# Attention + bilinear feed-forward on one core: the attention output of batches 2 to 7 is made token by token, in steps spread over units and outputs

## The chip, the cores and the metric

The kernel runs on one core of one Trainium2 chip. The metric is the device time in microseconds (us). Ten runs of the kernel before have a median of 322.74 us (321.78 to 323.73). Engines are named as in the profile: PE (TensorE), DVE (VectorE), ACT (ScalarE), POOL (GpSimd) and SP (SyncE, which here issues DMAs only).

## The reference

```python
# q, k, v: 8 batches, 8 heads, 576 tokens, 64 each; fp32
kv  = einsum('bhsd,bhse->bhde', k, v)
o   = einsum('bhsd,bhde->bhse', q, kv)
rms = sqrt(mean(o * o, axis=-1, keepdims=True) + 1e-6)     # over the 64 of one head
x   = (o / rms * g_norm).transpose(0, 2, 1, 3).reshape(4608, 512)
out = ((x @ w_a) * (x @ w_b)) @ w_out                      # d_ff = 1536; out is fp32, 4608 x 512
```

## The kernel before

The 4608 tokens of x are cut into nine strips of 512, whose limits do not fall on those of the batches of 576. x is kept transposed, features on partitions, in four tiles `xt[p]` of 128 features x 4608 tokens in bf16.

A strip has twelve *units* and four *outputs*. A unit (`class Unit`, `ffn_ab`) makes 128 of the 1536 hidden features for 512 tokens. `part_a` is four matmuls of 512 columns with w_a into one PSUM bank, which ACT copies to SBUF; `part_b` is four matmuls with w_b into another bank, which DVE multiplies by that copy (L273) into the tile `ab`. An output (`ffn_o`) is twelve matmuls of 512 columns for 128 tokens, an eviction by ACT or DVE in turn, and a store issued on SP. The banks of units rotate over 0, 1 and 2; even outputs use bank 3 (`O`).

The order of the work is written by hand: the program issues instructions in the order in which each engine's queue gets them. Strip 0 is preceded by the attention of batch 0 and followed by that of batch 1. In strip s (1 to 6) the attention of batch b = s + 1 is put between units and outputs by `slot(A, s, n)`, called once after unit or output n (n is 0 to 11 for units, 12 to 15 for outputs). Its steps for one batch are:

- `kv` (L158): k transposed times v, forty small matmuls into bank 7, and `kv_out`, two ACT copies that make the block-diagonal `kvb`, two heads in each of four blocks. It comes after unit 5 in strips 1 and 2, after unit 2 in later strips.
- for each of four pairs of heads p: `x` (L235), two matmuls of 288 columns with `kvb` as weights, into banks 4 and 5; `psq` (L205), the square on ACT; one slot later `pss`, two matmuls of 288 columns with a matrix of ones, which sum the squares over each head and spread the sum over its 64 features (L209), and the reciprocal root on ACT (L213); `pst` (L223), two DVE operations that write `xt`.

q reaches the kernel transposed in this way: `load_late(b)` issues, on POOL, the loads of batch b: q in bf16 to a scratch tensor `qs` in DRAM, then k and v to SBUF. Before it stands a copy of one element, `gate` (L126), which waits until the q of the batch before is transposed. `transpose_q(b)` (L141) is one DMA transposition on SP from `qs` to `qT[b % 2]`. `gate_d`, a DMA of one element of v of batch 1, holds back SP until the early loads are through.

`load_late(3)` is called after unit 8 of strip 1, `transpose_q(3)` and `load_late(4)` at that strip's end; in later strips `transpose_q(b + 1)` and `load_late(b + 2)` after unit 8. `transpose_q(2)` comes at the end of the attention of batch 1, behind the stores of strip 0.

Of the kernel before, what the change touches and what calls it, by code (L numbers as in the profile page):

```python
# [8 lines left out]
FP32 = mybir.dt.float32  # L9
BF16 = mybir.dt.bfloat16  # L10
AF = mybir.ActivationFunctionType
# [4 lines left out]
def kernel(  # L16
# [11 lines left out]
    nc = tc.nc  # L28

    B, H, S, D = q.shape  # L30
    d_model = H * D
    n_tok = B * S
    d_ff = moe_w_a.shape[1]
    KC = d_model // 128
    FC = d_ff // 128
    NP = H // 2
    HF = S // 2
    STRIP = 512
# [3 lines left out]
    EC, EP = 6, 96  # L42
# [6 lines left out]
    def sb(shape, dt, name):  # L49
        return pool.tile(shape, dt, name=name, tag=name)  # L50
# [17 lines left out]
    kvs = [sb([128, NP, D], BF16, f"kvs{i}") for i in range(2)]  # L68

    kvb = [sb([128, NP, 128], BF16, f"kvb{i}") for i in range(2)]  # L70
    xt = [sb([128, n_tok], BF16, f"xt{i}") for i in range(KC)]
    abt = [[sb([128, STRIP], BF16, f"ab{i}_{f}") for f in range(FC)] for i in range(2)]
    a_sb = [sb([128, STRIP], BF16, f"asb{i}") for i in range(4)]
    sq = [sb([128, 2, HF], BF16, f"sq{i}") for i in range(3)]
    rs = [sb([128, 2, HF], FP32, f"rs{i}") for i in range(3)]
    o_sb = [sb([128, d_model], FP32, f"osb{i}") for i in range(4)]
    o_end = sb([128, d_model // 2], FP32, "o_end")
    ident = sb([128, 128], BF16, "ident")
# [2 lines left out]
    g_col = sb([128, 1], FP32, "g_col")  # L81
    eps_t = sb([128, 1], FP32, "eps_t")
    warm = sb([128, 1], FP32, "warm")
    k32 = sb([EP, 2, EC, D], FP32, "k32")
    v32 = sb([EP, 2, EC, D], FP32, "v32")
    q32 = sb([EP, 2, EC, D], FP32, "q32")

    qc = sb([EP, EC, 2 * D], BF16, "qc")
    kc0 = sb([EP, EC, 2 * D], BF16, "kc0")
# [5 lines left out]
    P = psum.tile([128, 8, STRIP], FP32, name="P", tag="P")  # L95
    O = 3
# [26 lines left out]
    def load_late(b):  # L123
        if b > EARLY:

            nc.gpsimd.tensor_copy(gate, qT[(b - 1) % 2][0:1, 0, 0:1])  # L126
        d = qs_d[b].rearrange("t (h d) -> t h d", h=H)
        for hs in (slice(0, NP), slice(NP, H)):
            nc.gpsimd.dma_start(out=d[:, hs, :], in_=q[b, hs].rearrange("h t d -> t h d"))  # L129
        n = 128 * LC  # L130
        for t, src in ((ktl[b % 2], k), (vtl[b % 2], v)):
            nc.gpsimd.dma_start(
                out=t[:, :, 0:LC, :],
                in_=src[b, :, 0:n].rearrange("h (t c) d -> t h c d", c=LC),
            )
            nc.gpsimd.dma_start(
                out=t[0 : S - n, :, LC, :], in_=src[b, :, n:].rearrange("h t d -> t h d")
            )

    def transpose_q(b):  # L140
        nc.sync.dma_start_transpose(qT[b % 2], qs_d[b])  # L141


    class Attn:
# [75 lines left out]
        def pst(self, p, x0, hs=(0, 1)):  # L220
            for h in hs:
                t0 = self.b * S + h * HF
                nc.vector.scalar_tensor_tensor(  # L223
                    out=xt[p][:, t0 : t0 + HF],
                    in0=P[:, x0 + h, 0:HF],
                    scalar=g_col,
                    in1=rs[p % 3][:, h, :],
                    op0=ALU.mult,
                    op1=ALU.mult,
                )  # L230
# [10 lines left out]
                )  # L241


    class Unit:
        n = 0

# [5 lines left out]
        def mm(self, w, kcs):  # L252
            t0 = self.s * STRIP
            for kc in kcs:
                nc.tensor.matmul(  # L255
                    self.a if w is wa_t else self.b,
                    lhsT=w[:, kc, self.fc * 128 : (self.fc + 1) * 128],
                    rhs=xt[kc][:, t0 : t0 + STRIP],
                    start=(kc == KORD[0]),
                    stop=(kc == KORD[-1]),  # L260
                )
# [13 lines left out]
        def rest(self, kcs=KORD):  # L275
            self.part_a(kcs)
            self.part_b(kcs)

    n_ab = [0]

    def ffn_ab(s, fc):
        i = n_ab[0]
        n_ab[0] += 2
        Unit(s, fc, i % 3, (i + 1) % 3).rest()

    def store(t0, t, e0, e1, eng=nc.sync):
        i = 0
# [15 lines left out]
    def o_mm(s, g, i, fcs, e0=0, e1=d_model):  # L303
        for fc in fcs:
            nc.tensor.matmul(  # L305
                P[:, i, e0:e1],
                lhsT=abt[s % 2][fc][:, g * 128 : (g + 1) * 128],
                rhs=wo_t[:, fc, e0:e1],
                start=(fc == 0),
                stop=(fc == FC - 1),  # L310
            )

    def o_out(s, g, i):
        n = n_o[0]
        n_o[0] += 1
        t = o_sb[n % 4]
        if n % 2:
            nc.scalar.copy(t, P[:, i, :])  # L318
        else:
            nc.vector.tensor_copy(t, P[:, i, :])  # L320
        store(s * STRIP + g * 128, t, 0, d_model)

    def ffn_o(s, g, i=O):
        o_mm(s, g, i, range(FC))
        o_out(s, g, i)


# [41 lines left out]
    X, SS = (4, 0), 6  # L369


    A = Attn(0)
# [9 lines left out]
    t = P[:, 2, :].bitcast(BF16)[:, 0:S].rearrange("q (c t) -> q c t", c=EC)  # L382
# [4 lines left out]
    for c in range(EC):  # L387
        nc.tensor.matmul(
            P[:, SS, 0 : 2 * D],
            lhsT=kc0[:, c, :],  # L390
            rhs=vc[:, c, :],
            start=(c == 0),
            stop=(c == EC - 1),
# [10 lines left out]
    for p in range(1, NP):  # L404
        i = X[p % 2]
# [34 lines left out]
    u3.part_a()  # L440
    u2.part_b()
    u3.part_b()
    n_ab[0] = 1
    for fc in range(4, FC):
        ffn_ab(0, fc)


    A = Attn(1)
    h1, h2 = range(0, FC // 2), range(FC // 2, FC)

    nc.sync.dma_start(out=gate_d, in_=vt[1][0:1, H - 1, EC - 1, D - 1 : D])
    ffn_o(0, 0, X[0])
    pieces = [(1, h1), (1, h2), (2, h1), (2, h2), (3, h1), (3, h2)]
    for n, (g, fcs) in enumerate(pieces):
# [9 lines left out]
        if n < NP:  # L464
# [1 line left out]
            A.kv1(n, 2)  # L466
            A.kv_out(n, P[:, 2, STRIP - D :])
            A.qtr_out(n, 2)
    transpose_q(2)
    u0 = Unit(1, 0, 2, 3)  # L470
    u1 = Unit(1, 1, 4, 5)
    u0.first((0, 1, 2))
    u1.first((0, 1, 2))
    u0.rest((3,))
    u1.rest((3,))
    n_ab[0] = 0


    def slot(A, s, n):

        kb = P[:, 7, 0 : NP * D].rearrange("q (p e) -> q p e", e=D)
        k0, kn, xs = (5, 1, (7, 9, 11, 13)) if s < 3 else (2, 1, (4, 7, 10, 12))
        if k0 <= n < k0 + kn:
            for p in range((n - k0) * NP // kn, (n - k0 + 1) * NP // kn):
                A.kv(p, kb[:, p, :])
            if n == k0 + kn - 1:
                A.kv_out(slice(0, NP), kb)
        for p in range(NP):
            if n == xs[p]:
                A.x(p, X[0])  # L490
                A.psq(p, X[0])
            if n == xs[p] + 1:
                A.pss(p, SS)
                A.pst(p, X[0])

    for s in range(1, N_STRIP - 1):
        b = s + 1
        A = Attn(b) if b < B else None
        for n in range(FC + 4):
            if n >= FC:  # L500
                i = O if n % 2 == 0 else n_ab[0] % 3
                n_ab[0] += n % 2
                ffn_o(s, n - FC, i)
            elif s > 1 or n > 1:
                ffn_ab(s, n)
            if A:
                slot(A, s, n)
            if n == 8 and b + 1 < B:
                if s > 1:
                    transpose_q(b + 1)  # L510
                    if b + 2 < B:
                        load_late(b + 2)
                else:
                    load_late(3)
        if s == 1:
            transpose_q(3)
            load_late(4)
    last = N_STRIP - 1
    for fc in range(FC):
        ffn_ab(last, fc)  # L520
    for g in range(3):
        ffn_o(last, g, (O, 4)[g % 2])
# [38 lines left out]
```

## Time and profile before

| | |
|---|---|
| median of ten runs | 322.74 us |
| the profiled execution | 322.97 us |
| its span, first to last instruction | 321.2 us |
| granted TensorE clock | 0.999 |
| strips 3, 4, 5, 6: start on PE (us) | 119.97, 153.87, 187.77, 221.67 |
| strip 7 (no attention), strip 8: start on PE | 255.56, 286.64 |
| loads of q, k, v of batch 2: issued on POOL | 41.4 to 48.0 |
| kv step of batch 2 on PE | 61.06 to 62.9 |

The profile is one execution, with times in microseconds from the span's first instruction unless ns is written. A group's row joins instructions of one line of the code, one engine and one operation; `out<-in` are the program's tiles. A timeline's row joins neighbouring instructions of one kind: start, length, what, how many, and in brackets how long the engine had been idle and who ended that. The row of a matmul is longer than the time it keeps the next one waiting, since matmuls overlap. Weight loads (PEld) overlap them too. "q" after an engine's name means its queue, so `SPq` rows are DMA issues.

### The profile page before, as it was taken

The numbers are of one execution on the slowest core, as the hardware profiler recorded it, in microseconds if no ns is written. First come the engines' busy times: TensorE is split into PE (matmuls) and PEld (weight loads), VectorE is DVE, ScalarE is ACT, GpSimd is POOL, SyncE is SP. The second block draws the span as 40 slices with busy tenths as digits, with TensorE's granted clock in tenths as the row PEclk, the third lists the DMA queues.
The fourth block names the chain that finished last, engine by engine and source line by source line (L and its number), as shares of the span: only waits on it lengthen the run. The fifth ranks groups of instructions, "written<-read, shape, count | busy, mean of one in ns | idle before, by whom it ended". The sixth has DMA issues, their size and how long they took to land.

```text
span 321.2 us, 4697 instructions
## 1 busy us (share of the span) xinstructions
PE 312.9 (97%) x1848; PEld 150.6 (47%) x1883; DVE 124.9 (39%) x218; ACT 125.8 (39%) x217; POOL 70.0 (22%) x94
## 2 busy tenths in 40 slices
PE   8899999899999999999999999999999999999995
PEld 3444454444445444444444445444444444444443
DVE  5543344344234433453244323532354243313421
ACT  3733165353335424552355325533454233123310
POOL 8945890070034080160080000000000000000000
PEclk9999999999999999999999999999999999999999
DMA  8999999999359999999799141003000200020002
GB/s 177 196 196 199 200 181 226 142 83 162 89 94 148 147 113 211 102 112 174 142 67 156 65 119 23 0 35 99 0 2 0 98 35 0 23 90 22 0 33 98
DMA packets 79308, 32.60 MB, mean 101 GB/s; under 512 B 49974, under 2 KB 74806, under 8 KB 79286
## 3 DMA queue, kind: packets, MB, share of 16 engines
q0 software_dynamic: 59120, 18.44, 52.7%
q1 hardware_dynamic: 19810, 13.44, 17.8%
q10 hardware_dynamic: 356, 0.43, 0.4%
q8 instruction: 14, 0.23, 0.3%
q14 instruction: 8, 0.07, 0.1%
HBM read 37.75 MB, written 12.98 MB: 158 GB/s over the span
## 4 chain that ended last, share of the span: by engine, by line
PE 79%; DMA 14%; POOL 5%; issue 1%; ACT 0%; POOLq 0%
PE P L255 48%; PE P L305 26%; DMA wb_t<-in_moe_w_b_dram 6%; DMA vtl<-in_v_dram 5%; PE P L235 2%; PE P L209 2%; DMA qt<-in_q_dram 2%; DMA wo_t<-in_moe_w_out_dram 2%; PE P L158 1%; POOL qs L129 1%; POOL vt L106 1%; POOL wo_t L121 0%; POOL wb_t L360 0%; POOL wa_t L360 0%; POOL qt L106 0%
## 5 line engine op out<-in xcount | busy, mean ns | idle before, releaser
L273 DVE TENSOR_TENSOR ab<-P,asb 128x512 bf16<-128x512 f32 x108 | 74.5, 692 | 125.0 <-PE P L255 124.1
L255 PE MATMUL P<-xt,wa_t 128*128 128x512 bf16 x420 | 110.7, 379 | 1.0 <-issue 0.2
L255 PE MATMUL P<-xt,wb_t 128*128 128x512 bf16 x421 | 110.1, 379 | 0.4
L305 PE MATMUL P<-wo_t,ab 128*128 128x512 bf16 (+1 forms) x433 | 97.3, 373 | 0.6
L269 ACT CAST asb<-P 128x512 bf16<-128x512 f32 x108 | 63.1, 587 | 81.7 <-PE P L255 80.2
L255 PEld LDWEIGHTS <-wb_t 128*128 128x128 bf16 x432 | 42.3, 98 | 51.0 <-DMA wb_t<-in_moe_w_b_dram 0.3
L305 PEld LDWEIGHTS <-ab 128*128 128x128 bf16 x444 | 43.0, 98 | 45.6
L255 PEld LDWEIGHTS <-wa_t 128*128 128x128 bf16 x432 | 41.7, 98 | 44.7 <-issue 0.5
L223 DVE SCALAR_TENSOR_TENSOR xt<-P,g_col,rs 128x288 bf16<-128x288 f32 x64 | 30.1, 512 | 24.4 <-ACT rs L213 24.4
L213 ACT ACTIVATE rs<-P,eps_t 128x576 f32<-128x576 f32 (+1 forms) x33 | 23.9, 727 | 20.7 <-PE P L209 16.5
L318 ACT COPY osb<-P 128x512 f32<-128x512 f32 x17 | 10.0, 586 | 48.6 <-PE P L305 46.8
L205 ACT ACTIVATE sq<-P 128x576 bf16<-128x576 f32 x31 | 20.2, 651 | 20.2 <-PE P L235 18.2
L320 DVE COPY osb<-P 128x512 f32<-128x512 f32 x18 | 12.5, 692 | 32.4 <-PE P L305 32.3
L129 POOL DMA_DIRECT2D qs<-in_q_dram x12 | 19.6, 1635 | 2.2 <-issue 2.1
L126 POOL COPY gate<-qT 1x1 bf16<-1x1 bf16 x5 | 0.9, 177 | 85.4 <-DMA qT<-qs 85.4
L209 PE MATMUL P<-sq,ones 128*128 128x288 bf16 x64 | 13.2, 286 | 0.5 <-ACT sq L205 0.4
L235 PE MATMUL P<-qT,kvb 128*128 128x288 bf16 x56 | 11.9, 286 | 0.0
L169 ACT CAST kvb<-P 64x256 bf16<-64x256 f32 (+1 forms) x20 | 6.0, 301 | 12.4 <-PE P L158 12.3
L209 PEld LDWEIGHTS <-ones 128*128 128x128 bf16 x64 | 6.2, 98 | 7.4 <-issue 0.4
L235 PEld LDWEIGHTS <-kvb 128*128 128x128 bf16 x56 | 5.5, 98 | 6.0
L121 POOL DMA_DIRECT2D wo_t<-in_moe_w_out_dram x12 | 6.4, 530 | 6.7 <-DMA wb_t<-in_moe_w_b_dram 3.3
L330 PE MATMUL P<-zeros 128*128 128x512 bf16 x16 | 6.3, 542 | 1.2 <-DVE eps_t L345 1.2
(55 smaller groups left out, 83.7 us busy)
## 6 DMA issues: line engine op xcount, KB each, us to landing
out_dram<-osb SPq DMA_DIRECT2D x23, 256.0 KB, 2.0
qs<-in_q_dram POOLq DMA_DIRECT2D x12, 288.0 KB, 6.9
ktl<-in_k_dram POOLq DMA_DIRECT2D x6, 512.0 KB, 8.9
vtl<-in_v_dram POOLq DMA_DIRECT2D x6, 512.0 KB, 11.3
out_dram<-osb SPq DMA_DIRECT2D x13, 128.0 KB, 2.5
wo_t<-in_moe_w_out_dram POOLq DMA_DIRECT2D x12, 128.0 KB, 6.0
wa_t<-in_moe_w_a_dram POOLq DMA_DIRECT2D x5, 256.0 KB, 9.1
wb_t<-in_moe_w_b_dram POOLq DMA_DIRECT2D x5, 256.0 KB, 9.7
```

Of the source, the lines that this page charges most:

```text
L129: nc.gpsimd.dma_start(out=d[:, hs, :], in_=q[b, hs].rearrange("h t d -> t h d"))
L205: nc.scalar.activation(sq[p % 3], P[:, i0 : i0 + 2, 0:HF], AF.Square)
L209: nc.tensor.matmul(P[:, i0 + h, 0:HF], lhsT=ones, rhs=sq[p % 3][:, h, :], start=True, stop=True)
L213: nc.scalar.activation(rs[p % 3][:, h0:h1, :], P[:, i0 + h0 : i0 + h1, 0:HF], AF.Abs_reciprocal_sqrt, bias=eps_t,)
L223: nc.vector.scalar_tensor_tensor(out=xt[p][:, t0 : t0 + HF], in0=P[:, x0 + h, 0:HF], scalar=g_col, in1=rs[p % 3][:, h, :], op0=ALU.mult, o ...
L235: nc.tensor.matmul(P[:, i0 + h, 0:HF], lhsT=kvb[self.b % 2][:, p, :], rhs=self.qT[:, p, h * HF : (h + 1) * HF], start=True, stop=True,)
L255: nc.tensor.matmul(self.a if w is wa_t else self.b, lhsT=w[:, kc, self.fc * 128 : (self.fc + 1) * 128], rhs=xt[kc][:, t0 : t0 + STRIP], st ...
L269: nc.scalar.copy(self.t, self.a)
L273: nc.vector.tensor_mul(abt[self.s % 2][self.fc], self.b, self.t)
L305: nc.tensor.matmul(P[:, i, e0:e1], lhsT=abt[s % 2][fc][:, g * 128 : (g + 1) * 128], rhs=wo_t[:, fc, e0:e1], start=(fc == 0), stop=(fc == F ...
L318: nc.scalar.copy(t, P[:, i, :])
L320: nc.vector.tensor_copy(t, P[:, i, :])
```

## The change

Of batches 2 to 7, x is made by tokens. A batch has five chunks: four of 128 tokens and one of 64. A chunk c has four steps:

- `tx`: four matmuls of 128 columns, with 128 tokens of `qT` as weights and a block of `kvb` as the moving side. They fill one bank (5, 6 or 7, by c % 3) with tokens on partitions and all 512 features in the columns. ACT squares the bank into `sqt`.
- `tss`: DVE sums the squares of each head: 128 x 512 to 128 x 8.
- `trs`: ACT makes 128 x 8 reciprocal roots; POOL multiplies root and `g_norm`, both broadcast, to 128 x 512 in fp32, over `sqt`.
- `txt`: DVE multiplies the bank by that into a bf16 tile with tokens on partitions; SP issues a DMA transposition of it to `xt`, which is now one tile of 128 x 4 x 4608.

The matmuls with ones and the two DVE operations per pair are no longer used for these batches. A slot is now also called in the middle of a unit, between `part_a` and `part_b`, with n - 0.5, and in the middle of an output. A chunk that starts at x has its steps at x, x + 0.5, x + 1 and x + 2.5. In strip 1 the starts are 6.5, 7.5, 8.5, 9.5 and 10.5; in later strips 3.5, 5, 6, 7.5 and 8.5. kv of batch 3 (strip 2) moves from unit 5 to unit 2.

Units use four banks in turn (4, 1, 2, 0), and odd outputs take from the same rotation. `transpose_q(2)` moves ahead of strip 0's first output, so on SP ahead of that strip's stores; `transpose_q(3)` from the end of strip 1 to its first output; `load_late(3)` from unit 8 to unit 3 of strip 1; the other late loads to n = 13, the second output. Tiles for loads of the first heads (`k32`, `q32`, `v32`) lend their memory to the new tiles.

```diff
+    AB = (4, 1, 2, 0)
     n_ab = [0]
-    def ffn_ab(s, fc):
-        i = n_ab[0]
-        n_ab[0] += 2
-        Unit(s, fc, i % 3, (i + 1) % 3).rest()
+    def ab_bank():
+        n_ab[0] += 1
+        return AB[(n_ab[0] - 1) % len(AB)]
+
+    def ffn_ab(s, fc, between=None):
+        u = Unit(s, fc, ab_bank(), ab_bank())
+        u.part_a()
+        if between:
+            between()
+        u.part_b()
...
+        def tx(self, c, i):
+            t0 = c * 128
+            n = min(128, S - t0)
+            for p in range(NP):
+                nc.tensor.matmul(
+                    P[0:n, i, p * 128 : (p + 1) * 128],
+                    lhsT=self.qT[:, p, t0 : t0 + n],
+                    rhs=kvb[self.b % 2][:, p, :],
+                    start=True,
+                    stop=True,
+                )
+            nc.scalar.activation(
+                sqt[c % 3][0:n], P[0:n, i, :].rearrange("t (h d) -> t h d", h=H), AF.Square
+            )
+
+        def tss(self, c):
+            n = min(128, S - c * 128)
+            nc.vector.reduce_sum(sst[c % 3][0:n], sqt[c % 3][0:n], axis=mybir.AxisListType.X)
+
+        def trs(self, c):
+            n = min(128, S - c * 128)
+            nc.scalar.activation(
+                rst[c % 3][0:n],
+                sst[c % 3][0:n],
+                AF.Abs_reciprocal_sqrt,
+                bias=eps_t[0:n],
+                scale=1.0 / D,
+            )
+            nc.gpsimd.tensor_mul(
+                sqt[c % 3][0:n],
+                rst[c % 3][0:n].unsqueeze(2).to_broadcast([n, H, D]),
+                g_all[0:n].unsqueeze(1).to_broadcast([n, H, D]),
+            )
+
+        def txt(self, c, i):
+            t0 = c * 128
+            n = min(128, S - t0)
+            t = x_tok[c // 3][:, c % 3]
+            nc.vector.tensor_mul(
+                t[0:n], P[0:n, i, :].rearrange("t (h d) -> t h d", h=H), sqt[c % 3][0:n]
+            )
+            t0 += self.b * S
+            nc.sync.dma_start_transpose(
+                xt[:, :, t0 : t0 + n], t[0:n].rearrange("t h d -> t (h d)")
+            )
...
     nc.sync.dma_start(out=gate_d, in_=vt[1][0:1, H - 1, EC - 1, D - 1 : D])
+    nc.sync.dma_start(out=g_all, in_=g_norm.partition_broadcast(128))
+    transpose_q(2)
     ffn_o(0, 0, X[0])
...
-    transpose_q(2)
...
-        k0, kn, xs = (5, 1, (7, 9, 11, 13)) if s < 3 else (2, 1, (4, 7, 10, 12))
+        k0, xs = (5, (6.5, 7.5, 8.5, 9.5, 10.5)) if s == 1 else (2, (3.5, 5, 6, 7.5, 8.5))
...
-        for p in range(NP):
-            if n == xs[p]:
-                A.x(p, X[0])
-                A.psq(p, X[0])
-            if n == xs[p] + 1:
-                A.pss(p, SS)
-                A.pst(p, X[0])
+        for c, x in enumerate(xs):
+            i = 5 + c % 3
+            if n == x:
+                A.tx(c, i)
+            elif n == x + 0.5:
+                A.tss(c)
+            elif n == x + 1:
+                A.trs(c)
+            elif n == x + 2.5:
+                A.txt(c, i)
...
         for n in range(FC + 4):
+            amid = (lambda n=n: slot(A, s, n - 0.5)) if A else None
             if n >= FC:
-                i = O if n % 2 == 0 else n_ab[0] % 3
-                n_ab[0] += n % 2
-                ffn_o(s, n - FC, i)
+                ffn_o(s, n - FC, ab_bank() if n % 2 else O, amid)
             elif s > 1 or n > 1:
-                ffn_ab(s, n)
+                ffn_ab(s, n, amid)
             if A:
                 slot(A, s, n)
-            if n == 8 and b + 1 < B:
-                if s > 1:
-                    transpose_q(b + 1)
-                    if b + 2 < B:
-                        load_late(b + 2)
-                else:
-                    load_late(3)
-        if s == 1:
-            transpose_q(3)
-            load_late(4)
+
+            if s == 1 and n == 3:
+                load_late(3)
+            if b + 1 < B and n == (12 if s == 1 else 8):
+                transpose_q(b + 1)
+            if b + 2 < B and n == 13:
+                load_late(b + 2)
```

More of the change, by code (lines that the diff above doesn't have):

```diff
@@ L70 @@
     kvb = [sb([128, NP, 128], BF16, f"kvb{i}") for i in range(2)]
-    xt = [sb([128, n_tok], BF16, f"xt{i}") for i in range(KC)]
+    xt = sb([128, KC, n_tok], BF16, "xt")
     abt = [[sb([128, STRIP], BF16, f"ab{i}_{f}") for f in range(FC)] for i in range(2)]
@@ L75 @@
     rs = [sb([128, 2, HF], FP32, f"rs{i}") for i in range(3)]
+    k_x = sb([128, 2 * EC * D], FP32, "k_x")
+    k32 = k_x[0:EP].rearrange("p (h c d) -> p h c d", h=2, c=EC)
+    sqt = [sb([128, H, D], FP32, f"sqt{i}") for i in range(2)]
+    sqt.append(k_x[:, 0 : H * D].rearrange("p (h d) -> p h d", h=H))
+    sst = [sb([128, H], FP32, f"sst{i}") for i in range(3)]
+    rst = [sb([128, H], FP32, f"rst{i}") for i in range(3)]
+    g_all = sb([128, D], FP32, "g_all")
     o_sb = [sb([128, d_model], FP32, f"osb{i}") for i in range(4)]
@@ L83 @@
     warm = sb([128, 1], FP32, "warm")
-    k32 = sb([EP, 2, EC, D], FP32, "k32")
-    v32 = sb([EP, 2, EC, D], FP32, "v32")
-    q32 = sb([EP, 2, EC, D], FP32, "q32")
+    qv = [sb([128, 2 * EC * D], FP32, f"qv{i}") for i in range(2)]
+    q32, v32 = (t[0:EP].rearrange("p (h c d) -> p h c d", h=2, c=EC) for t in qv)
+    x_tok = [t.bitcast(BF16).rearrange("p (c h d) -> p c h d", c=3, h=H) for t in qv]
     qc = sb([EP, EC, 2 * D], BF16, "qc")
@@ L223, in pst @@
                 nc.vector.scalar_tensor_tensor(
-                    out=xt[p][:, t0 : t0 + HF],
+                    out=xt[:, p, t0 : t0 + HF],
                     in0=P[:, x0 + h, 0:HF],
@@ L257, in mm @@
                     lhsT=w[:, kc, self.fc * 128 : (self.fc + 1) * 128],
-                    rhs=xt[kc][:, t0 : t0 + STRIP],
+                    rhs=xt[:, kc, t0 : t0 + STRIP],
                     start=(kc == KORD[0]),
@@ L321, in o_out, with ffn_o @@
         store(s * STRIP + g * 128, t, 0, d_model)
-    def ffn_o(s, g, i=O):
-        o_mm(s, g, i, range(FC))
+    def ffn_o(s, g, i=O, between=None):
+        o_mm(s, g, i, range(FC // 2))
+        if between:
+            between()
+        o_mm(s, g, i, range(FC // 2, FC))
         o_out(s, g, i)
@@ L442 @@
     u3.part_b()
-    n_ab[0] = 1
+    n_ab[0] = 0
     for fc in range(4, FC):
@@ L475 @@
     u1.rest((3,))
-    n_ab[0] = 0
+    n_ab[0] = 1
     def slot(A, s, n):
         kb = P[:, 7, 0 : NP * D].rearrange("q (p e) -> q p e", e=D)
-        k0, kn, xs = (5, 1, (7, 9, 11, 13)) if s < 3 else (2, 1, (4, 7, 10, 12))
-        if k0 <= n < k0 + kn:
-            for p in range((n - k0) * NP // kn, (n - k0 + 1) * NP // kn):
+        k0, xs = (5, (6.5, 7.5, 8.5, 9.5, 10.5)) if s == 1 else (2, (3.5, 5, 6, 7.5, 8.5))
+        if n == k0:
+            for p in range(NP):
                 A.kv(p, kb[:, p, :])
-            if n == k0 + kn - 1:
-                A.kv_out(slice(0, NP), kb)
-        for p in range(NP):
-            if n == xs[p]:
-                A.x(p, X[0])
-                A.psq(p, X[0])
-            if n == xs[p] + 1:
-                A.pss(p, SS)
-                A.pst(p, X[0])
+            A.kv_out(slice(0, NP), kb)
+        for c, x in enumerate(xs):
[8 more added lines that the diff above has]
+                A.txt(c, i)
     for s in range(1, N_STRIP - 1):
```

## The prediction

> **What bounds the kernel now.** I read the page's engine shares and costliest groups first. Columns of a group: line, engine, operation, output and inputs, count, then busy us, mean ns of one, then idle us of the engine before them and what ended most of it.
>
> ```profile
> PE 312.9 (97%) x1848; PEld 150.6 (47%) x1883; DVE 124.9 (39%) x218; ACT 125.8 (39%) x217; POOL 70.0 (22%) x94
> ...
> L273 DVE TENSOR_TENSOR ab<-P,asb 128x512 bf16<-128x512 f32 x108 | 74.5, 692 | 125.0 <-PE P L255 124.1
> ...
> L209 PE MATMUL P<-sq,ones 128*128 128x288 bf16 x64 | 13.2, 286 | 0.5 <-ACT sq L205 0.4
> L235 PE MATMUL P<-qT,kvb 128*128 128x288 bf16 x56 | 11.9, 286 | 0.0
> ```
>
> TensorE (PE) is busy nearly all the time; VectorE and ScalarE idle mostly because they wait for it. The waits of PE alone, longest first, say that it waits for almost nothing:
>
> ```profile
> PE P L330 <- DVE eps_t L345: 1.2, 1, 1.2
> PE P L158 <- DMA vtl<-in_v_dram: 0.9, 1, 0.9
> PE P L209 <- ACT sq L205: 0.4, 1, 0.4
> ```
>
> The 0.4 lies in the prologue; the 0.9 is the kv step of batch 2, in strip 1. Nothing waits in the later strips, so there each matmul taken off PE is time gained, until something else becomes late. A table of stretches shows it: strips 5 and 6, which carry attention, and strip 7, which carries none (columns: stretch, its length, busy us and count of PE, weight load, DVE, ACT, POOL, then clock, DMA share, GB/s).
>
> ```profile
> 187.77:221.67 33.90, 33.69 (x198) 16.26 (x201) 13.45 (x22) 14.41 (x24) 0.00 (x0) 1.00 0.18 45
> 221.67:255.57 33.90, 33.69 (x198) 16.28 (x201) 13.45 (x22) 14.41 (x24) 0.00 (x0) 1.00 0.10 36
> 255.57:286.68 31.11, 30.95 (x143) 14.10 (x145) 9.68 (x14) 8.22 (x14) 0.00 (x0) 1.00 0.09 35
> ```
>
> Attention of one batch costs 33.90 - 31.11 = 2.79 us, all of it PE time. The timeline gives the pieces (columns: start, length, engine, line):
>
> ```profile
> 7.06 0.49 PE L388 MATMUL P<-vc,kc 96*128 96x128 bf16 x6
> ...
> 54.14 1.29 DVE L273 TENSOR_TENSOR ab<-P,asb 128x512 bf16<-128x512 f32 x2 [1.46 <-PE P L255]
> ...
> 58.28 1.03 PE L255 MATMUL P<-xt,wb_t 128*128 128x512 bf16 x4
> ...
> 59.42 0.69 DVE L273 TENSOR_TENSOR ab<-P,asb 128x512 bf16<-128x512 f32 x1 [1.04 <-PE P L255]
> ```
> ```profile
> 247.31 0.41 PE L235 MATMUL P<-qT,kvb 128*128 128x288 bf16 x2
> 247.55 2.75 PE L305 MATMUL P<-wo_t,ab 128*128 128x512 bf16 x11
> 250.14 0.41 PE L209 MATMUL P<-sq,ones 128*128 128x288 bf16 x2
> 250.38 5.34 PE L305 MATMUL P<-wo_t,ab 128*128 128x512 bf16 x24
> ```
>
> A matmul's own duration (286 ns) is not its price, since matmuls overlap; the price is the distance to the next start. Two 288-column matmuls take 247.55 - 247.31 = 0.245 us, so 0.1225 each (0.24 for the ones, too). Six 128-column matmuls, each with its own weight load, span 0.49 with a mean of 0.218: five distances of (0.49 - 0.218) / 5 = 0.055. For 512 columns the distance is 1.726 us per unit / 8 = 0.216.
>
> **What the skill says.** "TensorE: Matmul & The Clock Gate", section "Back-to-back issue gap", gives N / 2.4 + 2.5 ns for the distance, which the three numbers above meet within 1 ns; the same section warns of about 81 ns at N = 128 in a stream of load and matmul pairs. The six pairs above say 55; I take 55 and keep 81 as the upper end. "GPSIMD Engine Reference", section "Elementwise — side-by-side cycle accounting", has 4497 ns for a two-input product of 2048 fp32 per partition; a quarter is an estimate of 1.12 us. This trace shows no such operation; the nearest, the mask of 128 elements made on POOL in the prologue (287 ns), gives 1.15 times four.
>
> **The change, part by part.**
>
> *x by tokens.* Removed per batch: 8 x matmuls and 8 matmuls with ones, 16 x 0.1225 = 1.96 us. Added: 5 chunks x 4 matmuls x 0.055 = 1.10 us. Six batches: 6 x 0.86 = 5.16 us off PE (with 81 ns it would be 6 x 0.34 = 2.0). The weight loads grow from 16 to 20 per batch, and hide behind the matmul before, as in the row of six.
>
> *The other engines' work.* Per strip DVE gives up 8 x 0.512 and takes 5 sums and 5 products, each over as many elements as the ab product (0.69): +2.8 on 13.45 in a strip of 33. ACT gives up 4 x (0.651 + 0.742) and takes 5 squares (0.59, as the copies of 128x512) and 5 small roots (0.2, as the first activation): -1.6. POOL takes 5 products, 5.6 us. All of it lies beside PE; it costs only if one step comes too late for the next user of its bank. So I follow the bank chain.
>
> *Strips 2 to 6.* With 0 at the end of part_a of unit 5, ACT has the root at 1.0, POOL's first product ends at 2.2, DVE reaches txt(0) after the product of unit 6, about 3.7: POOL is early by 1.5. tx(3) uses the bank of chunk 0 and stands 1.5 units after txt(0); tx(4) one unit after txt(1), which DVE ends about 1.1 us ahead of it. No wait on PE. The cover is thin only for POOL (below).
>
> *Strip 1.* Here the chunks start at 6.5, 7.5, 8.5, 9.5, 10.5, one unit apart. txt(0) is due at 9, tx(3) at 9.5, only half a unit later, in the same bank. With 0 at the end of unit 9's matmuls: DVE starts the ab product at 0.28 (59.42 less 58.28 + 4 x 0.216), the second operation of a pair follows 0.60 later (1.29 - 0.69), txt(0) ends at 0.28 + 0.60 + 0.69 = 1.57, and PE gets it about 0.06 later. PE is through part_a of unit 10 at 0.86. It stands for 1.63 - 0.86 = 0.77 us, and nothing else can go on PE. tx(4) meets txt(1) in the same way. Two waits: +1.54 us. Bounds: 0 if DVE were far faster, 3 if POOL is late too.
>
> *Earlier transposition of q of batch 2.* In the SP queue it now stands ahead of the eight stores of strip 0's outputs.
>
> ```profile
> 46.68 5.89 SPq L298 DMA_DIRECT2D out_dram<-osb  x8
> ```
> ```profile
> 62.29 0.69 PE L158 MATMUL P<-vtl,ktl 128*64 128x64 bf16 x32 [0.92 <-DMA vtl<-in_v_dram]
> ...
> 63.61 0.18 POOL L126 COPY gate<-qT 1x1 bf16<-1x1 bf16 x1 [15.57 <-DMA qT<-qs]
> 64.45 3.26 POOL L129 DMA_DIRECT2D qs<-in_q_dram  x2 [0.67 <-issue]
> ...
> 70.13 0.72 POOL L136 DMA_DIRECT2D vtl<-in_v_dram  x1
> ```
>
> The transposition started at 53.80, after the stores, though its source was issued by 43.26 with 6.9 us median to landing, so about 50.2. The skill ("Trainium Kernel Development and Optimization", "Key Constraints") has all queues share the same 16 DMA engines; here the v load, issued at 46.4, took 14.7 us against 11.3 for the median of all v loads. With the stores behind, it should land earlier. Of the 0.92 I take 0.7 as gained (between 0 and 0.92). The stores go out by about 66; their buffers are next written at 77.
>
> *Loads of batch 3* (n = 3 instead of 8) follow the gate, thus the transposition, not their place: POOL was idle for 15.57 before. But POOL products now stand behind these issues. Issuing takes 63.61 to 70.85; if the gate opens 3 us earlier it ends by about 67.5, when the first root comes out (unit 8 of strip 1). *Transposition of batch 3* at n = 12: SP reaches it near 79, its source landed by 73; it lands near 85 and the loads of batch 4 are issued by 92, ahead of strip 2's first product near 95. From strip 3 on the transposition of q waits behind two chunk transposes, later by some 10 us; everything it feeds is due a strip later. *kv of batch 3* at unit 2: needed near 90, loaded by 80. Cost 0 each.
>
> *Chunk transposes on SP.* A q transposition of 576 rows took 2.4 to 6.9 us to issue and at most 10.6 to land; a chunk has 128. The tightest is chunk 2 in strip 1, due 10.4 us (four outputs) after unit 11, less 1.6 for DVE. Between 0 and 1.8; I take 0.
>
> *Four ab banks, halves of outputs.* PE did not wait for a bank before; 0.
>
> Sum against the profiled execution (322.97, span 321.2): -5.16 + 1.54 - 0.7 = -4.3, so 318.65; the median of the runs is 0.23 lower, so 318.4.
>
> **Rivals.**
>
> A. No wait in strip 1 (DVE runs earlier than I have it), kv wait gone: 322.74 - 5.86 = 316.9. Against it: three measured durations leave 0.77. Chance 0.08.
>
> B. The gate of batch 3 does not open earlier. POOL issues until 70.85, its first product ends at 71.95, txt(0) at 72.7, while PE stands at tx(3) from 71.4: 1.35 instead of 0.77, and the kv wait stays: -5.16 + 2.12 = -3.0, 319.7. For it: the shared DMA engines are full there. Chance 0.15.
>
> C. 81 ns for each of 120 short matmuls: +3.1 on the forecast, 321.5. For it, the skill's sentence; against it, the row of six. Chance 0.08, half of it within 0.3% of before.
>
> D. Slower: the POOL product is several times its estimate, and DVE stands at txt with the ab products queued behind it. In strips 2 to 6, with 0 as above, txt(1) is through at 1.06 + 2T + 0.75, and PE wants its bank for tx(4) at 7.56 (the matmuls from part_b of unit 5 to part_a of unit 9). PE waits from T = 2.9 us and the batch's gain of 0.86 is gone at T = 3.3; at T = 4 it costs 2.25 x 5 = 11.3 us, thus 329.7. For it: no such product is in the trace, and its inputs are broadcast. Chance 0.10.
>
> **How the numbers follow.** The main case has 0.59. A measurement of this kernel tells about 0.3% (1 us) from no change. Faster: 0.59 + 0.08 + 0.15 + 0.04 = 0.86; within: 0.04; slower: 0.10. The range 316.8 to 320.8 holds the main case with its bounds, A and B, and leaves out C and D, 0.18.
>
> **What would show it.** Strips 3 to 6 should last 33.90 - 0.86 = 33.0 us with no PE wait; the token matmuls should stand 55 ns apart; PE should show two waits of about 0.8 us for a DVE product that writes x by tokens, both in strip 1; the POOL product should last about 1.1 us; the wait for v at batch 2's kv should shrink. I am wrong if strips 3 to 6 show waits of PE for DVE, if the distance is nearer 80, or if the POOL product is over 2.9.

## The result, and the profile after

The kernel after takes 319.20 us (median; 319.12 to 320.08), the kernel before 322.76 in the same series: a ratio of 0.9895, interval 0.988 to 0.9909. Its profiled execution took 319.15 us (span 317.4), 3.82 less than that of before. The forecast was 318.4 in a range of 316.8 to 320.8. The sign and the mechanism hold, and 0.8 us of the gain is missing: 0.5 against the profiled executions (319.15 where 318.65 was forecast), the rest because the forecast took off the 0.23 by which the profiled execution of before lay above the median, while that of after lies at its median.

From the page: shares of the engines, then two groups of the new steps, POOL's product in `trs` and the matmuls of `tx`.

```profile
PE 308.5 (97%) x1872; PEld 147.6 (46%) x1907; DVE 138.2 (44%) x230; ACT 115.7 (36%) x229; POOL 101.6 (32%) x124
...
L282 POOL TENSOR_TENSOR sqt<-rst,g_all 128x512 f32<-128x512 f32 (+1 forms) x24 | 25.0, 1042 | 97.4 <-ACT rst L275 97.4
...
L258 PE MATMUL P<-kvb,qT 128*128 128x128 bf16 (+1 forms) x120 | 11.7, 220 | 1.2 <-DVE qv L292 1.2
```

PE is still busy 97% of the span; DVE and POOL have taken up work, ACT has given some up. The unknown of the forecast, the POOL product, takes 1042 ns. The tile `qv` in these and later rows is `x_tok` (one memory), so L292 is the step `txt`, and L258 is `tx`.

The waits of PE, longest first (waited for, then total us, times, longest):

```profile
PE P L397 <- DVE eps_t L412: 1.2, 1, 1.2
PE P L258 <- DVE qv L292: 1.2, 2, 0.6
PE P L219 <- ACT sq L215: 0.4, 1, 0.4
```

The wait for v at the kv step of batch 2 (0.9 in the list of before) is gone; two waits for the DVE product that writes x by tokens have come. No row names `xt`, so no chunk transposition came too late.

Stretches of strips 1, 3 and 7 (length; busy us and count of PE, weight load, DVE, ACT, POOL; clock, DMA share, GB/s):

```profile
50.62:85.27 34.65, 33.27 (x202) 15.85 (x204) 16.60 (x27) 13.20 (x27) 11.80 (x12) 1.00 1.26 166
...
151.83:185.11 33.28, 33.07 (x202) 15.80 (x205) 15.70 (x24) 12.74 (x26) 11.83 (x12) 1.00 0.91 128
...
251.66:282.74 31.08, 30.92 (x142) 14.07 (x144) 9.68 (x14) 8.19 (x14) 0.00 (x0) 1.00 0.09 35
```

Strips 2 to 6 all last 33.28. Before, the first matmuls of units stood like this (lengths of strips on PE, us):

| strip | before | after | difference |
|---|---|---|---|
| 1 | 35.33 | 34.65 | -0.68 |
| 2 | 34.13 | 33.28 | -0.85 |
| 3, 4, 5, 6 | 33.90 each | 33.28 each | -0.62 each |
| 7, 8 | 31.08, 31.27 | 31.08, 31.27 | 0 |

These make -4.01; strip 1 starts 0.11 later. So the whole of the gain lies in the strips with attention, and a later strip gives 0.62 instead of the forecast 0.86. Attention of a batch now costs 33.28 - 31.08 = 2.20 us of PE, before 33.90 - 31.08 = 2.82 (the prediction's 2.79 took 31.11 for strip 7).

### The profile page after: what moved, and what is told of

Read it like the earlier page. It is cut to its first block, busy times and chain, and to the rows that moved or that the text cites. A ratio compares the mean times of both kernels' runs of the same rounds, so it can differ in the third digit from the quotient of the medians.

```text
span 317.4 us, 4944 instructions
## 1 busy us (share of the span) xinstructions
PE 308.5 (97%) x1872; PEld 147.6 (46%) x1907; DVE 138.2 (44%) x230; ACT 115.7 (36%) x229; POOL 101.6 (32%) x124
## 4 chain that ended last, share of the span: by engine, by line
PE 94%; ACT 2%; DMA 1%; issue 1%; DVE 1%; ACTq 0%; DVEq 0%
PE P L312 57%; PE P L369 29%; PE P L258 2%; PE P L168 2%; DMA qv<-in_q_dram 1%; ACT asb L326 1%; PE P L192 1%; PE P L219 1%; PE P L397 1%; PE P L206 0%; DVE qv L292 0%; ACT sq L215 0%; PE P L245 0%; PE P L451 0%; DVE sst L271 0%
## 5 line engine op out<-in xcount | busy, mean ns | idle before, releaser
L369 PE MATMUL P<-wo_t,ab 128*128 128x512 bf16 (+1 forms) x433 | 95.0, 373 | 0.6
L282 POOL TENSOR_TENSOR sqt<-rst,g_all 128x512 f32<-128x512 f32 (+1 forms) x24 | 25.0, 1042 | 97.4 <-ACT rst L275 97.4
L271 DVE TENSOR_REDUCE sst<-sqt 128x8 f32<-128x512 f32 (+1 forms) x24 | 16.2, 676 | 0.8 <-ACT sqt L265 0.5
L292 DVE TENSOR_TENSOR qv<-P,sqt 128x512 bf16<-128x512 f32 (+1 forms) x24 | 16.2, 678 | 0.0
L265 ACT ACTIVATE sqt<-P 128x512 f32<-128x512 f32 (+1 forms) x24 | 14.2, 594 | 1.6 <-PE P L258 1.6
L258 PEld LDWEIGHTS <-qT 128*128 128x128 bf16 (+1 forms) x120 | 8.9, 100 | 9.5 <-issue 4.0
L258 PE MATMUL P<-kvb,qT 128*128 128x128 bf16 (+1 forms) x120 | 11.7, 220 | 1.2 <-DVE qv L292 1.2
L275 ACT ACTIVATE rst<-sst,eps_t 128x8 f32<-128x8 f32 (+1 forms) x30 | 9.0, 301 | 4.3 <-DVE sst L271 4.3
L233 DVE SCALAR_TENSOR_TENSOR xt<-P,g_col,rs 128x288 bf16<-128x288 f32 x16 | 7.5, 511 | 5.2 <-ACT rs L223 5.2
L282 POOL TENSOR_TENSOR k_x<-rst,g_all 128x512 f32<-128x512 f32 x6 | 6.3, 1042 | 7.5 <-ACT rst L275 7.5
```

Of the source, the lines that this page charges most:

```text
L258: nc.tensor.matmul(P[0:n, i, p * 128 : (p + 1) * 128], lhsT=self.qT[:, p, t0 : t0 + n], rhs=kvb[self.b % 2][:, p, :], start=True, stop=True,)
L265: nc.scalar.activation(sqt[c % 3][0:n], P[0:n, i, :].rearrange("t (h d) -> t h d", h=H), AF.Square)
L271: nc.vector.reduce_sum(sst[c % 3][0:n], sqt[c % 3][0:n], axis=mybir.AxisListType.X)
L282: nc.gpsimd.tensor_mul(sqt[c % 3][0:n], rst[c % 3][0:n].unsqueeze(2).to_broadcast([n, H, D]), g_all[0:n].unsqueeze(1).to_broadcast([n, H, D]),
L292: nc.vector.tensor_mul(t[0:n], P[0:n, i, :].rearrange("t (h d) -> t h d", h=H), sqt[c % 3][0:n])
L369: nc.tensor.matmul(P[:, i, e0:e1], lhsT=abt[s % 2][fc][:, g * 128 : (g + 1) * 128], rhs=wo_t[:, fc, e0:e1], start=(fc == 0), stop=(fc == F ...
```

## Where 0.24 us of every strip went

PE does not wait in strips 2 to 6, so the loss must lie in its own instructions. PE's timeline in strip 3, the last two chunks (start, length, line, how many):

```profile
134.75 0.39 PE L258 MATMUL P<-kvb,qT 128*128 128x128 bf16 x4
134.98 1.03 PE L312 MATMUL P<-xt,wb_t 128*128 128x512 bf16 x4
135.84 1.03 PE L312 MATMUL P<-xt,wa_t 128*128 128x512 bf16 x4
136.80 0.41 PE L258 MATMUL P<-kvb,qT 128*64 128x128 bf16 x4
137.14 1.04 PE L312 MATMUL P<-xt,wb_t 128*128 128x512 bf16 x4
```

Four 512-column matmuls take 4 x 0.216 = 0.864 us from start to start. The full chunk before takes 134.98 - 134.75 = 0.23 (0.22 in most places), and no gap lies ahead of it: 55 ns for each matmul, as forecast. The chunk of 64 tokens has weights of 64 columns (`128*64`). It starts 136.80 - (135.84 + 0.864) = 0.10 late, with no wait in brackets, and takes 0.34 instead of 0.22. Together 0.22 us more than a full chunk, for half its tokens. The weight loads of the same stretch (PEld), the first for the full chunk:

```profile
134.54 0.42 PEld L258 LDWEIGHTS <-qT 128*128 128x128 bf16 x4
...
136.80 0.25 PEld L258 LDWEIGHTS <-qT 128*64 128x64 bf16 x4 [0.42 <-issue]
137.14 0.55 PEld L312 LDWEIGHTS <-wb_t 128*128 128x128 bf16 x4
```

The loads of the full chunk begin at 134.54, 0.21 ahead of its first matmul (134.75) and so beside the matmul before it. At the change to 64 columns and at the change back, the first load begins only together with its matmul, at 136.80 and at 137.14: it is not hidden there. The theory after the result was therefore: going from 128-column weights to 64-column ones and back costs about 0.1 each way, and this is the mis-sized term. The rival was that any short chunk at this place, or the waits on banks and buffers around it, costs the same.

In strip 1 both kinds of loss are seen, DVE and PE in order of time:

```profile
69.41 1.03 PE L312 MATMUL P<-xt,wa_t 128*128 128x512 bf16 x4
...
70.29 0.68 DVE L292 TENSOR_TENSOR qv<-P,sqt 128x512 bf16<-128x512 f32 x1
...
71.03 0.38 PE L258 MATMUL P<-kvb,qT 128*128 128x128 bf16 x4 [0.59 <-DVE qv L292]
...
72.11 1.03 PE L312 MATMUL P<-xt,wa_t 128*128 128x512 bf16 x4
...
73.72 0.38 PE L258 MATMUL P<-kvb,qT 128*64 128x128 bf16 x4 [0.59 <-DVE qv L292]
```

PE is through part_a at 69.41 + 0.864 = 70.27, DVE's product `txt` runs from 70.29 to 70.97, and `tx` of chunk 3 starts at 71.03: it stood for 0.76. At chunk 4, 73.72 - 72.11 - 0.864 = 0.75. The brackets say 0.59, because they count from the end of a matmul's record, which lasts about 0.16 longer than the distance to the next start (379 against 216 ns).

## The experiments

Ratios are to the kernel before, timed on the same chip: 322.58 us beside the first four, 322.35 beside the POOL product made three times, 322.73 beside the others.

**Strip 1 with spaced chunks.** Only the starts of strip 1 change, so that chunks 3 and 4 come a unit later.

```diff
-        k0, xs = (5, (6.5, 7.5, 8.5, 9.5, 10.5)) if s == 1 else (2, (3.5, 5, 6, 7.5, 8.5))
+        k0, xs = (5, (6.5, 7.5, 8.5, 10.5, 11.5)) if s == 1 else (2, (3.5, 5, 6, 7.5, 8.5))
```

> Only strip 1's last two chunks move, from 9.5 and 10.5 to 10.5 and 11.5, so that each stands 1.5 units after the product that frees its bank. Theory: the two stops of PE in strip 1 (0.75 us each) come from the half unit between txt and tx alone; both go, 319.2 - 1.5 = 317.7, and no PE wait for the token product is left. Rival: POOL or the sums are late in strip 1 anyway, and the waits move along: 318.7 to 319.2.

317.72 us, ratio 0.9847 (0.9829 to 0.9866). Strip 1 lasts 33.28, like the others. Its timeline where the first wait was:

```profile
70.07 0.68 DVE L292 TENSOR_TENSOR qv<-P,sqt 128x512 bf16<-128x512 f32 x1
...
71.78 0.39 PE L258 MATMUL P<-kvb,qT 128*128 128x128 bf16 x4
```

The bank is free at 70.75, a microsecond before `tx` needs it at 71.78. Strip 1 gains 34.65 - 33.28 = 1.37 us: the two waits of 0.75, less the gap ahead of the 64-token chunk, which had lain inside the second wait. Nothing became late in their place.

**The last chunk with 128 tokens.** It takes tokens 448 to 575 instead of 512 to 575; the 64 that chunk 3 has already made are computed again and not transposed again.

```diff
-            t0 = c * 128
-            n = min(128, S - t0)
+            t0 = min(c * 128, S - 128)
+            n = 128
...
+            n, r = 128, c * 128 - t0
...
-                xt[:, :, t0 : t0 + n], t[0:n].rearrange("t h d -> t (h d)")
+                xt[:, :, t0 + r : t0 + n], t[r:n].rearrange("t h d -> t (h d)")
```

> The last chunk takes 128 tokens (448 to 575) instead of 64; the 64 that chunk 3 has too are computed twice and written once. As many matmuls, on full 128-column weights. Theory: the last chunk's 0.44 us, against 0.22 of the others, is the price of going to 64-column weights and back (0.09 before, 0.05 inside, 0.12 after, as at the kv step); about 0.22 per strip goes in strips 2 to 6 and 0.1 to 0.2 in strip 1: 319.2 - 1.2 = 318.0. Rival: the extra comes from its place in the middle of a unit: no change, 319.2.

317.98 us, 0.9853 (0.9834 to 0.9871). Strips 2 to 6 last 33.05. PE at the last chunk of strip 2:

```profile
102.51 1.03 PE L312 MATMUL P<-xt,wa_t 128*128 128x512 bf16 x4
103.37 0.39 PE L258 MATMUL P<-kvb,qT 128*128 128x128 bf16 x4
103.59 1.03 PE L312 MATMUL P<-xt,wb_t 128*128 128x512 bf16 x4
```

Twice the columns in the weights, and it starts without the 0.10 (102.51 + 0.864 = 103.374) and takes 0.22 instead of 0.34. Place, bank and buffer are the same, so the rival is out: the 64-column weights are the cause. The loads above show where the time lies, at the two changes of width, where the first load does not run ahead; why it does not, no run here shows.

**Both.**

> Both edits. Theory: they are independent and add up: 319.2 - 1.5 - 1.2 = 316.5, with strips 1 to 6 all about 33.05 us long. Rival: one hides the other, 317.5 or more.

316.27 us, 0.9809 (0.979 to 0.9828): the two edits add, and this version beats both kernels. Its strip 1:

```profile
50.49:83.55 33.06, 33.06 (x207) 15.82 (x204) 16.52 (x27) 13.22 (x27) 12.40 (x14) 1.00 1.36 180
```

PE is busy in the whole of the stretch. Strips 2 to 6 last 33.05, what the forecast wanted of strips 3 to 6 (33.0).

**q of batch 2 transposed late again**, at its old place behind the stores of strip 0; all else as after.

```diff
-    transpose_q(2)
     ffn_o(0, 0, X[0])
...
+    transpose_q(2)
```

> One part undone: the transposition of q of batch 2 goes back behind strip 0's stores on SP. Theory: the v load of batch 2 lands late again, the kv step waits about 1 us as before the change, the gate of batch 3 opens some 3 us later, POOL still issues loads when the first product is due, and the first wait in strip 1 grows by about 0.6: 319.2 + 1.2 to 1.8 = 320.4 to 321.0. Rival: the order on SP does not matter for the loads: 319.2.

320.66 us, 0.9943 (0.9924 to 0.9962). POOL and PE in strip 1:

```profile
62.97 0.18 POOL L136 COPY gate<-qT 1x1 bf16<-1x1 bf16 x1 [15.12 <-DMA qT<-qs]
...
70.19 2.08 POOL L282 TENSOR_TENSOR sqt<-rst,g_all 128x512 f32<-128x512 f32 x2
...
72.06 0.38 PE L258 MATMUL P<-kvb,qT 128*128 128x128 bf16 x4 [1.41 <-DVE qv L292]
```

In the kernel after the gate opens at 60.32 and POOL's first product starts at 67.52. Here the gate opens at 62.97, the loads of batch 3 occupy POOL until 70.21, the product waits behind them, and PE stands for 0.82 more at `tx` of chunk 3 (1.41 against 0.59). The kv step waits for v again (0.3 in brackets; from `part_b` to the next unit 2.22 us pass instead of 1.71). Strip 1 lasts 35.99, 1.34 more. This is the chain of the prediction's rival B: it exists, and the move of one DMA keeps it away.

**The kernel before with only that move.**

```diff
+    transpose_q(2)
     ffn_o(0, 0, X[0])
...
-    transpose_q(2)
```

> One part alone: the kernel before, with only the transposition of q of batch 2 moved ahead of strip 0's outputs. Theory: the wait at batch 2's kv goes (0.92 idle, about 1.1 with the weight loads after it), nothing else moves: 322.75 - 1.1 = 321.65. Rival: the earlier transposition takes DMA time from the loads of k and v, and the wait stays: 322.75.

321.91 us, 0.9973 (0.9959 to 0.9988), about 0.8 below the kernel before. v lands at 59.24 instead of 62.25, and the kv step runs without a wait. PE around it, in the kernel before and then with the move:

```profile
60.01 1.03 PE L255 MATMUL P<-xt,wb_t 128*128 128x512 bf16 x4
61.06 0.32 PE L158 MATMUL P<-vtl,ktl 128*64 128x64 bf16 x8
...
62.92 1.04 PE L255 MATMUL P<-xt,wa_t 128*128 128x512 bf16 x3
```
```profile
60.24 1.03 PE L255 MATMUL P<-xt,wb_t 128*128 128x512 bf16 x4
61.20 0.82 PE L158 MATMUL P<-vtl,ktl 128*64 128x64 bf16 x40
61.95 1.04 PE L255 MATMUL P<-xt,wa_t 128*128 128x512 bf16 x4
```

From one unit's `part_b` to the next unit 62.92 - 60.01 = 2.91 us pass before and 61.95 - 60.24 = 1.71 with the move, and strip 1 goes from 35.33 to 34.13. The wait was thus worth 1.2, where the list of waits had 0.92. The difference is again one of counting: the bracket begins at the end of a matmul's record, 0.20 long here, while the starts in this step are (0.82 - 0.20) / 39 = 0.016 apart, which makes 0.18; and the step's first matmul came 0.09 late as well (61.06, where 60.97 is usual), since the larger load of v landed only at 61.02.

**The POOL product made two, three and four times** (it is repeated over the same output; the time per chunk was 2.17, 3.28 and 4.41 us). This moves T, the quantity on which the slower rival D turned.

```diff
-            nc.gpsimd.tensor_mul(
+            for _ in range(2):
+                nc.gpsimd.tensor_mul(
```

> The POOL product is made twice per chunk, 2.08 instead of 1.04 us. Theory: below the 2.9 us from which PE should wait in strips 2 to 6, so 319.2, at most 0.5 more in strip 1. Rival: POOL is nearly on the path and each added us shows in every strip: 320.5 or more.

318.99 us, 0.9868 (0.9824 to 0.9911): strips as in the kernel after. Twice the product is still hidden.

> The POOL product is made three times per chunk; by the run with four (4.4 us) that is T = 3.3 us. Theory: just past the 2.9 us from which PE should wait at tx(4); 2 x 3.3 + 1.81 - 7.56 = 0.85 us in each of strips 2 to 6, 4.3 us, and up to 2 us more in strip 1, and no stretch of PE at half clock: 323.5 to 325.5. Rival: what made four products cost 38 us (stops at outputs, half clock) is there too: over 328.

326.75 us, 1.0127 (1.01 to 1.0155), 1.25 above the upper end. PE's waits (the loop has shifted the lines by one):

```profile
PE P L258 <- DVE qv L293: 5.6, 7, 1.1
...
PE P L370 <- DVE osb L385: 1.1, 5, 0.2
```

At chunk 4 of a later strip PE stood 174.98 - (173.29 + 0.864) = 0.83 us, where 2 x 3.28 + 1.81 - 7.56 = 0.81 comes from the prediction's formula. What was missing is the second row: an output's bank, evicted by DVE, comes free late, because the eviction stands in DVE's queue behind `txt`, which waits for POOL. It costs 0.39 per strip by the distances of starts. Strips 2 to 6 last 34.45, 1.17 more than after.

> The POOL product is made four times per chunk, 4.17 us. Theory: beyond the 2.9 us; the second product of a batch ends 2 x 4.17 + 1.06 after the start, PE waits 2 x 4.17 + 1.81 - 7.56 = 2.6 us at tx(4) in each of strips 2 to 6, 13 us, and about 3 us more at tx(3), tx(4) of strip 1: 332 to 338. Rival: DVE, queued behind, passes the delay on to the units as well: over 340; or the slack is larger than worked out: under 328.

357.34 us, 1.1061 (1.1009 to 1.1114), far above both expectations. PE in strip 4:

```profile
190.22 0.38 PE L258 MATMUL P<-kvb,qT 128*64 128x128 bf16 x4 [2.25 <-DVE qv L293]
...
192.86 1.91 PE L313 MATMUL P<-xt,wb_t 128*128 128x512 bf16 x4
194.57 1.28 PE L313 MATMUL P<-xt,wa_t 128*128 128x512 bf16 x4
...
203.88 2.32 PE L370 MATMUL P<-wo_t,ab 128*128 128x512 bf16 x10 [1.35 <-DVE osb L385]
```

A strip is 6.79 longer than after. The waits for `txt` make 0.66 + 2.42 = 3.08, where the formula has 2 x 4.41 + 1.81 - 7.56 = 3.07: that part was right. Later in the strip, outputs wait 0.63 and 1.51 (0.47 and 1.35 in brackets), and matmuls run at half speed: the four from 192.86 take 194.57 - 192.86 = 1.71 us, 0.427 each, twice 0.216. From 191.41 to the start at 195.69, twelve matmuls take 4.28 instead of 2.59.

The half speed does not make the strip longer, however. Strips 2 and 4 (the clock stands behind the five busy times):

```profile
88.86:128.92 40.06, 33.97 (x205) 15.76 (x204) 16.84 (x26) 12.73 (x26) 34.58 (x35) 1.00 0.98 125
168.99:209.06 40.07, 35.50 (x206) 16.16 (x205) 15.62 (x24) 12.74 (x26) 27.19 (x28) 0.96 0.69 101
```

Strip 2 ran at full clock throughout and is as long as strip 4; PE stood still in it for the time that it computed slowly in strip 4. Strip 5 is like strip 2, and strips 3 and 6 like strip 4. What they share is POOL's row of products. With four products per chunk, POOL in strip 4 and then DVE at the row's end:

```profile
180.68 8.77 POOL L283 TENSOR_TENSOR sqt<-rst,g_all 128x512 f32<-128x512 f32 x8 [11.69 <-ACT rst L275]
189.40 4.41 POOL L283 TENSOR_TENSOR k_x<-rst,g_all 128x512 f32<-128x512 f32 x4
193.77 8.74 POOL L283 TENSOR_TENSOR sqt<-rst,g_all 128x512 f32<-128x512 f32 x8
...
202.54 0.68 DVE L293 TENSOR_TENSOR qv<-P,sqt 64x512 bf16<-64x512 f32 x1 [3.05 <-POOL sqt L283]
203.15 0.67 DVE L385 COPY osb<-P 128x512 f32<-128x512 f32 x1
```

With three:

```profile
167.68 6.52 POOL L283 TENSOR_TENSOR sqt<-rst,g_all 128x512 f32<-128x512 f32 x6 [11.69 <-ACT rst L275]
174.16 3.28 POOL L283 TENSOR_TENSOR k_x<-rst,g_all 128x512 f32<-128x512 f32 x3
177.40 6.50 POOL L283 TENSOR_TENSOR sqt<-rst,g_all 128x512 f32<-128x512 f32 x6
```

The products of the five chunks follow each other without a gap. After the last one come `txt` of chunk 4, the eviction queued behind it on DVE, and only then the output on PE (203.88). The rows last 202.51 - 180.68 = 21.83 and 183.90 - 167.68 = 16.22 us, 5.61 apart; the strips are 40.07 - 34.45 = 5.62 apart. So here the whole row of five sets the length of the strip, 5 us for each us of T, where the prediction's formula has 2. A strip less its row is 18.24 with four products and 18.23 with three, so a row fits into a strip of 33.28 up to about 15.04, that is, up to a T of 3.0 (an estimate from these two runs).

**Three banks for the units**, so that odd outputs and units rotate over 1, 2 and 0 as before, and bank 4 is unused.

```diff
-    AB = (4, 1, 2, 0)
+    AB = (1, 2, 0)
...
-    n_ab[0] = 1
+    n_ab[0] = 2
```

> Units rotate over three banks (1, 2, 0) as before the change; all else as after. Theory: the ab product is at most 0.7 us late behind a sum or a token product, which three banks still allow (0.8 us): 319.2 to 319.7. Rival: with the new DVE steps in between, three banks make PE wait for a bank several times a strip: 321 or more.

319.12 us, 0.9875 (0.984 to 0.991), strips as after. The fourth bank is worth nothing here.

## Why the prediction was right, and what it had wrong

By its own steps, against the profiled executions:

| step | forecast | measured | from |
|---|---|---|---|
| x by tokens, six batches | -5.16 | -3.86 | 0.62 in each of strips 2 to 6; about 0.76 in strip 1 (1.96 less its chunks, 4 x 0.22 and 0.32) |
| two waits in strip 1 | +1.54 | +1.50 | starts on PE, 0.75 each |
| wait for v of batch 2 | -0.7 | -1.20 | starts around the kv step |
| bank waits of before in strips 1 and 2 | not seen | -0.48 | rows of x, below |
| sum | -4.3 | -4.0 | strips: -4.0 |

The sum is nearer than its terms. The first promised 1.30 too much; the third was 0.50 too small, and 0.48 of gain was not forecast at all. That these errors nearly cancel is luck.

*x by tokens: right in kind, mis-sized.* The full chunks cost 55 ns per matmul, so the upper end of 81 (rival C) does not apply: the sentence on it in the Trainium skill ("TensorE: Matmul & The Clock Gate", section "Back-to-back issue gap") is not met by these 96 matmuls, each with a weight load, while that section's N / 2.4 + 2.5 ns is (55.8). They come in groups of four among 512-column matmuls; a long stream of short ones, of which the sentence speaks, was not run. The term that failed is "5 chunks x 4 matmuls x 0.055", which took the last chunk for a full one. In strips 2 to 6 it costs 0.44 instead of 0.22 because its weights have 64 columns; the run with a full last chunk shows it.

The same gap stands ahead of the kv step, whose weights have 64 columns too: in strip 1 of the kernel after, part_b starts at 60.12, so it is through at 60.98, and kv starts at 61.07 without a wait. It stands in the kernel before as well (strip 4: part_b starts at 158.19, so it is through at 159.05, and kv starts at 159.15), so the price could have been read there.

*Two waits in strip 1: right, to 0.04.* They follow from three durations and the order of DVE's queue; the spaced version, which has none, shows that they are avoidable, so what rival A hoped for (no wait) needs no faster DVE, only two other numbers in a list.

*q of batch 2: right, under-sized.* The transposition started at 50.21 (forecast 50.2). The wait went entirely, and it was worth 1.20 instead of the 0.92 in the list. In the kernel before the move is worth 0.8 to 1.2, in the kernel after 1.5 (320.66 - 319.2), where it also keeps POOL ahead of the roots. Cost on SP: none seen, the stores started at 57.41 as their queue allows and no buffer was late.

*Not seen: two stops of x in strips 1 and 2 of the kernel before.* A row of two x matmuls normally lasts 0.41 and takes 0.245 to the next start.

```profile
70.32 0.52 PE L235 MATMUL P<-qT,kvb 128*128 128x288 bf16 x2
70.69 1.02 PE L255 MATMUL P<-xt,wa_t 128*128 128x512 bf16 x4
```

Here it takes 0.37: the second half waits 0.12 for its bank inside a row, where no bracket shows it. It starts at 70.57, 0.05 after DVE's second operation on the pair before has released that bank (70.51). Two in each of the two strips, 0.48 in all. The forecast rested on strips 5 to 7, which have none; the strip lengths (34.13 for strip 2 against 33.90) would have told.

*The other engines' work: right.* DVE's sum and product take 676 and 678 ns (0.69 taken), POOL's product 1042 (1.12 estimated; the figure behind it, in the Trainium skill's "GPSIMD Engine Reference", section "Elementwise — side-by-side cycle accounting", is for a two-input add, not a product). Strip 3 has 2.25 us more of DVE's time than strip 5 before (2.8 forecast) and 1.67 less of ACT's (1.6). None of it makes PE wait in strips 2 to 6, even with the POOL product doubled. *Chunk transposes* were taken at nothing: right, none was late. *Loads of batch 3:* POOL's issuing ended at 67.55 (67.5 forecast). *Four banks:* nothing, as forecast.

*Rival D* did not come, since T is 1.04. Its point of decision was nearly right: no wait at 2.17, and at 3.28 the kernel is already slower than before, where the prediction had the gain gone at 3.3. Its price above that point was much too small, at T = 4.4 less than half (3.07 against 6.79 per strip): it priced the second product at `tx` alone and left out that all five stand in a row on POOL, with an eviction behind the last on DVE.

## What to carry to other kernels

Price a short matmul by the distance to the next start, but look separately at each one whose weights have another width than its neighbours': here a remainder tile of half the width cost twice a full one, and overlapping it with its neighbour, so that some work is done twice, was faster. When a step waits for another engine, add up that engine's whole row of work, and price all that is queued behind the step on its own engine, not only its direct consumer. And compare the lengths of stages that should be alike before any wait is read; the stops inside a row of two matmuls appeared in no list.

## What was not expected of the hardware

- A switch from 128-column to 64-column weights and back costs about 0.22 us of PE (0.10 ahead of the chunk, 0.12 from its start to the next unit), with no wait in the profile, in each of strips 2 to 6; it goes when the weights have 128 columns. At both changes the first weight load begins only with its matmul, instead of 0.21 ahead.
- With four POOL products, PE ran at half speed (0.427 us per 512-column matmul instead of 0.216) in strips 3, 4 and 6, after stops of 0.66 and 2.42 us with 2 us of work between them; the granted clock was 0.50 for 3.41 us each time, from 150.70, 191.66 and 270.17. The Trainium skill ("TensorE: Matmul & The Clock Gate", section "What's actually happening") puts the return to the lower clock after an idle window of about 3.4 us; here no stop was that long. The same two stops in strips 2 and 5 brought no lower clock, nor did stops of 2.87 and 2.42 in strip 1, nor those of up to 1.3 in the run with three products. The second and third slow stretches begin 40.96 and 119.47 us after the first, which is 12 and 35 times 3.413; so where a stop falls on such a grid may decide, but that was not tested.
- A POOL product with both inputs broadcast takes 1042 ns for 128 x 512 fp32, and nearly the same (1036) for 64 x 512. DVE working beside it does not slow it: in the run with four products, those during which DVE stood idle took 1042 too.
